# Delta-rule attention before a Fourier-mixing MLP: T V and L U on four array tiles, first blocks from key Gram products, a schedule that counts instruction blocks

## The chip, the cores and the metric

One core of one Trainium2 chip runs the whole program. The metric is device time in microseconds (us). TensorE (PE in the profile; PEld are its weight loads) multiplies, VectorE (DVE), ScalarE (ACT) and GpSimd (POOL) work on elements, and SyncE (SP) issues most DMAs. All data are float32. The profile has two records for each float32 matmul and one for each transpose by TensorE, and each record has a weight load beside it.

## What is computed

```python
# q, k, v: (4, 8, 768, 48); beta: (4, 8, 768); k_n = k / (norm(k) + 1e-6)
for t in range(768):                        # a state of 48 x 48 for each of 4 x 8 heads
    y[:, :, t] = q_t @ state
    state += beta_t * outer(k_n_t, v_t - k_n_t @ state)
x = y, the heads side by side               # (4, 768, 384)
u = x + real(fft(fft(x, axis=1), axis=2))
un = (u - mean(u)) / sqrt(var(u) + 1e-6)    # over the 384
out = u + relu(un @ w_ch1) @ w_ch2          # 384 -> 1536 -> 384
```

## The kernel before

**Units.** The recurrence is done in chunks of 64 tokens. A unit is 128 tokens (two chunks, c = 0 and 1, on partitions 0 to 63 and 64 to 127) of all 8 heads of one batch; 6 units make a batch and 24 the program. A head is h = 2j + s: j counts pairs, and s = 0 (even) or 1 (odd) tells on which half of the partitions the head lies once keys and queries are transposed. Units come in rounds: units 0 to 3, units 4 and 5 (these two rounds are the early ones, batch 0), and then four at a time.

**One unit.** `turn` (line 490) transposes keys and queries with eight 64x64 transposes each. `gram` (line 528) forms K K^T and K Q^T in chunks; the masked K Q^T is L. A triangular inverse T of the key products (with beta and the norms) is formed by row elimination on DVE over 32x32 blocks (`invert`, line 784) for a round at once, and `blocks` (line 814) joins the 32-blocks to 64. For the early rounds the elimination is over 16x16 blocks (`invert16`, line 704), and `join` (line 749) makes 32-blocks of them by matmuls. Their diagonal blocks come from `diag` (line 508), 32x32 products of the transposed keys, which DVE transposes straight out of PSUM in `begin16` (line 636). `ahead` (line 868) makes W^T = K^T T (the copy of `wt`) and U = T V (the copy of `u`). `step` (line 898), for each chunk, subtracts W S from U (DVE, line 922) and adds K^T U to the state S (DVE, line 943): this is the serial chain of a batch, 12 chunk steps long. `outputs` (line 949) sums Q S and L U in PSUM and moves it to `x` (two ACT copies, two DVE adds of line 996).

**Array tiles.** A matmul with 64 rows and 64 columns uses a quarter of the array: rows of half c or s, columns of the PSUM half that it writes. W^T, `gram` and the Q S part of `outputs` use all four quarters in turn. T V and L U use two: chunk c is read on half c and written on half c.

**After attention.** When a batch's last unit is out, `mixing` runs on it: `folds` (DVE), `seq` (matmuls with `tab`), `feat` (matmuls with `ft`, the mean and the variance), `normed` (transposes of `un`), and `mlp`, three groups of 256 tokens with 12 PE operations each of some 2.6 us (line 1172). Batch 0 has no earlier MLP beside its attention; batches 1 to 3 have that of the batch before. The float64 weights come as pairs of 32-bit words and are turned into float32 by ACT, DVE and POOL (`weights`, line 1222), through staging places in `xs[1]` and `R1`.

**Who sets the order.** `Plan` (line 40) collects all operations with a duration, their data dependencies, and a due time. `schedule` plays them through on a model of the engines (four PSUM slots, the DMA rate, the gated TensorE clock) and emits each engine's instructions in the order of that play; on the chip each engine works its list off in order. Between 35 and 123 us of the planned time, when recent TensorE columns are below `TARGET` per us, it lets only big matmuls in, or puts fillers into the list (`idle`, line 1437: a 128x128 by 128x256 matmul whose result nobody reads).

```python
LIM = {"attn": 3, "mix": 2, "mlp": 2}       # PSUM slots a class may hold, of four
t[a, 0, D * h:D * h + D]  <-  z.TT[a, h, :], z.V[a, h, :]     # T V: a = half c
t[a, c, D * h:D * h + D]  <-  z.LT[a, h, :], z.U[a, h, :]     # L U, added to Q S
```

Of the kernel before, what the change touches and what calls it, by code (L numbers as in the profile page):

```python
# [24 lines left out]
class Op:  # L25
    __slots__ = ("i", "engs", "fn", "deps", "succ", "pr", "mode", "banks", "new", "lat",
                 "ndep", "ready", "start", "end", "eng", "due", "kb", "col")


SHARE = 0.6  # L30
# [3 lines left out]
TARGET, SPANW = 350.0, 2.6  # L34


class Plan:
# [10 lines left out]
    def op(self, engs, fn, rd=(), wr=(), pr=0.0, mode=None, new=None, use=(), lat=0.0,  # L48
           due=1e9, kb=0, col=0):
# [4 lines left out]
        o.due, o.kb, o.col = due, kb, col  # L54
# [27 lines left out]
    def speed(self, now):  # L82
# [5 lines left out]
        return 2.0 if self.cold and CLOCK else 1.0  # L88

# [18 lines left out]
    def schedule(self, pick, limits, switch, idle=None, span=(0.0, 0.0)):  # L108
# [24 lines left out]
        self.win, self.sum, self.cold, self.past, self.hist = 0.0, 0.0, True, [], []  # L133
        done, n, now = 0, len(ops), 0.0
        order = []
        while done < n:
            progressed = False
            for e in self.ENG:
# [4 lines left out]
                if e == "PE":  # L143
# [4 lines left out]
                    low = span[0] <= now < span[1] and self.light(now)  # L148
                    if low:
                        cand = [o for o in cand if o.col > 1000]  # L150
# [6 lines left out]
                    if low and best is None and fr and idle:  # L157
                        best = Op()
                        best.i, best.fn, best.mode, best.deps = -1, idle(fr[0]), "128", set()
                        best.pr, best.lat, best.due, best.kb, best.col = 0.0, 0.0, 0.0, 0, 256  # L160
                        best.engs, best.new, best.banks, best.succ = {"PE": 0.22}, None, [], []
                        slots[fr[0]] = now + 0.3
                elif cand:
# [6 lines left out]
                    if best and LOOK and e in ("DVE", "ACT"):  # L170

                        x = now + best.engs[e] - HOLD
                        if any(now < o.ready[e] < x and o.pr < best.pr - LOOK for o in avail[e]
                               if e in o.engs and o is not best):
                            best = None
# [15 lines left out]
                if o.kb:  # L191
# [4 lines left out]
                    o.lat = landed[-1] - o.end  # L196
                free[e] = o.end
# [38 lines left out]
def _consts(S, DM):  # L236
# [10 lines left out]
    lo = (p % 32) >= 16  # L247
    pack = np.concatenate([ident, su, mk.reshape(128, 64), m01, lo[:, None]], axis=1)
# [32 lines left out]
def kernel(  # L281
# [41 lines left out]
    pack = sb("pack", 128 + 64 + 64 + 3)  # L323
# [39 lines left out]
    m16 = pack[:, 258:259]  # L363
    PK = A(pack, 0, 259)
# [6 lines left out]
    def I(x):  # L371
        kp(x)
# [64 lines left out]
    def unit(u):  # L437
# [25 lines left out]
        if u < GS + 2:  # L463
            g, go = w1, 3072 + 256 * u
            z.GF = g[:, go:go + 256].rearrange("p (h t) -> p h t", h=H)
            z.aGF = A(g, go, go + 256)
# [24 lines left out]
    def turn(z, pr, what=(1, 0), after=()):  # L491
# [3 lines left out]
        def fn(e):  # L495
            t = psum(b)
            for i, a in enumerate(what):
                w = (z.Q, z.K)[a].rearrange("p (j s) t -> p j (s t)", s=2)
                for j in range(NJ):
                    for c in range(2):  # L500
                        tr(t[:, c, 256 * a + 64 * j:256 * a + 64 * j + 64],
                           w[64 * c:64 * c + 64, j, :], 64 * c, 64, i == 0 and j == 0)
        rd = [PK] + [(A(z.q, 0, 512), z.aK())[a] for a in what] + list(after)
        P.op({"PE": 0.35 * len(what)}, fn, rd, [(z.aQT, z.aTT)[a]() for a in what], pr, "T",
             new=b, lat=LE, col=500)
        for a in what:
            def ev(e, a=a):
                copy(e, z.QK[:, a].rearrange("p e j t -> p e (j t)"),
                     psum(b)[:, :, 256 * a:256 * a + 256])
            P.op(either(512), ev, [], [(z.aQT, z.aTT)[a]()], pr - EV, use=[b], lat=LA)  # L510

    def diag(z, b, ul, pr):
# [961 lines left out]
```

## Time and profile before

| | us |
|---|---|
| median of 3 runs | 744.56 (744.11 to 747.56) |
| the profiled execution | 751.2 |
| its span in the trace | 749.1 |
| TensorE busy, share of the span | 695.9, 93% |
| VectorE busy | 404.6, 54% |
| ScalarE busy | 243.9, 33% |
| mean granted TensorE clock | 0.969 |
| fillers: records, busy | 102, 34.2 |
| first `join` matmul | 36.7 |
| first state step (`step`) | 63.3 |
| first matmul of batch 0's `seq` | 126.4 |
| first MLP matmul | 152.1 |

The profiled execution is one execution; its span lies inside its time. The profile shows the program by engine, by stretches of time, by the chain of work that ended last, and by groups of instructions under the line that issued them. Most matmuls are issued by the helper at line 375, transposes at 378 and copies at 384, so groups are told apart by the tiles that they read and write: `pp<-u,us` is U as moving operand (K^T U and L U), `pp<-st,us` is Q S, `pp<-us 64*64 64x48` is T V, `pp<-us 64*64 64x64` is W^T. "issue" is time in which an engine waited for nothing that the profile shows. A matmul's record has the time from its start to its modelled end, some 0.2 us, and the next record starts long before that end: the pace is read from how many start in a stretch.

### The profile page before, as it was taken

Reading aid. Unit: us, or ns where it says so; the run is one execution under the profiler, and the core shown is the slowest. Engines: PE = TensorE matmul, PEld = TensorE weight load, DVE = VectorE, ACT = ScalarE, POOL = GpSimd, SP = SyncE. Lnnn points to the kernel's source line nnn. Section 1 sums busy time; section 2 is a strip of 40 time slices with the busy share of each in tenths; the row PEclk is TensorE's granted clock in tenths of the full one; section 3 lists DMA queues with packets and bytes.
Section 4 is the critical chain, followed back from the end, with each engine's and each line's share of the span. In section 5 each row is a group of like instructions: output and inputs, shape, how many; then the busy total and the mean of one; then the engine's idle time right before and its main releaser. Section 6 shows DMA issues by size and latency. Waiting matters only on the chain.

```text
span 749.1 us, 22953 instructions
## 1 busy us (share of the span) xinstructions
PE 695.9 (93%) x10332; PEld 551.2 (74%) x10332; DVE 404.6 (54%) x1074; ACT 243.9 (33%) x546; POOL 28.5 (4%) x31
## 2 busy tenths in 40 slices
PE   4397999989899999898999999999999999999997
PEld 4276888877688676887778767778777677777774
DVE  1984559899533794469943589327992400600000
ACT  3163465633534113354144321255213110421110
POOL 2011211011100000000000000000000000000000
PEclk9998889999899999898999999999999999999999
DMA  9515242210222001320013200010000000000000
GB/s 197 171 27 144 50 111 40 69 57 28 80 67 55 11 21 37 64 55 1 0 25 77 45 11 22 11 46 14 2 1 24 1 22 0 22 1 1 21 22 21
DMA packets 82563, 31.34 MB, mean 42 GB/s; under 512 B 75553, under 2 KB 79618, under 8 KB 82338
## 3 DMA queue, kind: packets, MB, share of 16 engines
q1 hardware_dynamic: 82274, 29.65, 16.2%
q8 instruction: 81, 1.33, 0.8%
q10 hardware_dynamic: 192, 0.23, 0.1%
q14 instruction: 16, 0.13, 0.1%
HBM read 25.16 MB, written 4.72 MB: 40 GB/s over the span
## 4 chain that ended last, share of the span: by engine, by line
PE 68%; DVE 25%; issue 4%; ACT 2%; DMA 1%; SPq 0%; ACTq 0%; DVEq 0%
PE pp L375 62%; DVE rr L800 5%; DVE tmp L795 5%; PE pp L1437 4%; PE pp L378 2%; DVE rr L809 1%; DVE gd L812 1%; DVE pm L1017 1%; DVE un L1136 1%; DVE eo L1017 1%; DVE x L996 1%; ACT x L384 1%; DVE us L822 1%; DMA us<-in_k_dram 1%; DVE rr L610 1%
## 5 line engine op out<-in xcount | busy, mean ns | idle before, releaser
L375 PE MATMUL pp<-w,R 128*128 128x384 f32 x576 | 202.6, 498 | 0.0
L375 PE MATMUL pp<-R,w 128*128 128x256 f32 x864 | 200.6, 386 | 0.8 <-ACT R L384 0.8
L375 PEld LDWEIGHTS pp<-R,w 128*128 128x128 f32 x864 | 164.4, 193 | 30.1 <-ACT R L384 1.0
L375 PEld LDWEIGHTS pp<-w,R 128*128 128x128 f32 x576 | 108.3, 192 | 64.3 <-issue 3.6
L1186 ACT ACTIVATE R<-pp 128x512 f32<-128x512 f32 x72 | 43.0, 597 | 209.8 <-PE pp L375 204.7
L375 PE MATMUL pp<-us 64*64 64x48 f32 (+3 forms) x2368 | 73.2, 250 | 5.5 <-ACT us L384 3.5
L375 PEld LDWEIGHTS pp<-us 64*64 64x64 f32 (+2 forms) x2368 | 63.7, 142 | 13.6 <-issue 8.3
L1214 DVE TENSOR_TENSOR x<-x,pp 128x768 f32<-128x768 f32 x12 | 11.4, 951 | 108.6 <-PE pp L375 108.6
L384 ACT ACTIVATE us<-pp 128x512 f32<-128x512 f32 (+2 forms) x110 | 48.6, 463 | 49.3 <-PE pp L375 32.7
L375 PE MATMUL pp<-u,us 64*64 64x48 f32 x1360 | 57.1, 228 | 2.9 <-issue 2.5
L375 PEld LDWEIGHTS pp<-u,us 64*64 64x64 f32 x1360 | 50.6, 142 | 9.6 <-issue 8.0
L800 DVE TENSOR_TENSOR rr<-rr,tmp 128x30 f32<-128x30 f32 (+9 forms) x150 | 50.6, 337 | 4.4
L795 DVE TENSOR_TENSOR tmp<-rr 128x30 f32<-128x30 f32 (+9 forms) x150 | 50.4, 336 | 4.5
L922 DVE TENSOR_TENSOR u<-u,pp 64x384 f32<-64x384 f32 (+1 forms) x55 | 25.2, 471 | 50.5 <-PE pp L375 40.6
L943 DVE TENSOR_TENSOR st<-st,pp 128x192 f32<-128x192 f32 (+1 forms) x50 | 15.2, 312 | 52.3 <-PE pp L375 45.1
L384 ACT ACTIVATE x<-pp 64x384 f32<-64x384 f32 x48 | 23.3, 485 | 44.0 <-PE pp L375 43.7
L375 PE MATMUL pp<-tab,R 128*96 128x193 f32 (+2 forms) x192 | 35.8, 330 | 0.2 <-DVE x L996 0.2
L384 ACT ACTIVATE R<-pp 128x384 f32<-128x384 f32 (+7 forms) x66 | 23.7, 414 | 32.5 <-PE pp L375 19.7
L1437 PE MATMUL pp<-pack 128*128 128x256 f32 x102 | 34.2, 464 | 0.0
L375 PE MATMUL pp<-st,wt 48*64 48x48 f32 x704 | 32.5, 226 | 1.5 <-DVE st L943 0.7
L375 PEld LDWEIGHTS pp<-tab,R 128*96 128x96 f32 (+2 forms) x192 | 30.2, 163 | 3.6 <-issue 1.7
L375 PEld LDWEIGHTS pp<-st,wt 48*64 48x64 f32 x704 | 27.8, 139 | 6.3 <-issue 5.1
(124 smaller groups left out, 690.0 us busy)
## 6 DMA issues: line engine op xcount, KB each, us to landing
qt<-in_q_dram SPq DMA_DIRECT2D x24, 192.0 KB, 2.9
x<-in_moe_w_ch_dram SPq DMA_DIRECT2D x9, 512.0 KB, 4.4
out_dram<-x SPq DMA_DIRECT2D x12, 384.0 KB, 2.5
us<-in_v_dram SPq DMA_DIRECT2D x22, 192.0 KB, 3.0
us<-in_k_dram SPq DMA_DIRECT2D x22, 192.0 KB, 3.3
tab<-k_tab SPq DMA_DIRECT2D x1, 1155.0 KB, 8.0
R<-in_moe_w_ch_dram SPq DMA_DIRECT2D x3, 384.0 KB, 4.8
x<-in_moe_w_ch_dram SPq DMA_DIRECT2D x3, 384.0 KB, 3.2
```

Of the source, the lines that this page charges most:

```text
L375: I(nc.tensor.matmul(o, lhsT=lhsT, rhs=rhs, start=start, stop=stop, skip_group_check=True))
L378: I(nc.tensor.matmul(o, lhsT=src, rhs=ident[p0:p0 + n, p0:p0 + n], is_transpose=True, start=start, stop=True, skip_group_check=True))
L384: I(nc.scalar.activation(o, i, ACT.Copy, **({} if scale is None else {"scale": scale})))
L610: vec(1400, lambda e: I(nc.vector.transpose(R, ro.gd(0, 4).rearrange("p (n c) -> p c n", c=32))), [ro.agd(0, 4)], [aR], pr)
L795: I(eng(e).tensor_tensor(T_, R[:, :, j + 1:32, j:j + 1].broadcast_to([128, ns, n, j]), R[:, :, j:j + 1, 0:j].broadcast_to([128, ns, n, j]) ...
L800: I(eng(e).tensor_tensor(R[:, :, j + 1:32, 0:j], R[:, :, j + 1:32, 0:j], T_, op=ALU.add))
L922: I(nc.vector.tensor_tensor(U, U, psum(b1)[a, :, s0:s1].rearrange("p s (j d) -> p s j d", d=D), op=ALU.subtract))
L943: I(nc.vector.tensor_tensor(sn[:, s0:s1], so[:, s0:s1], psum(b2)[:, 0, s0:s1], op=ALU.add))
L1017: I(eng(e).tensor_tensor(o, i0, i1, op=op))
L1186: I(nc.scalar.activation(o, psum(bk)[:, :, 0:256], ACT.Relu))
L1214: I(nc.vector.tensor_tensor(w, w, psum(bk)[:, :, 0:DM], op=ALU.add))
L1437: I(nc.tensor.matmul(pst[slot][:, 0, 0:256], lhsT=pack[:, 0:128], rhs=pack[:, 0:256], start=True, stop=True, skip_group_check=True))
```

## The change

- **T V on four quarters.** An odd head's product is written to the other half of the partitions and to a second PSUM bank. U is then moved by three copies (even heads of both halves; the odd heads of each half back to their own half) where one did it before.
- **L U on four quarters.** In the same manner; the odd heads' sums lie apart from Q S, and `outputs` has two copies and three adds in place of two and two.
- **First blocks.** `diag` goes. `keys` makes the whole 64x64 key products of two units in 32 matmuls on four quarters, copies move the diagonal 32-blocks to `gd` (four copies of 32 partitions for two units), and `begin16` transposes from there. The off-diagonal part is kept, so the early rounds' `gram` makes K Q^T alone.
- **`join`** uses 64-row operands with zeros in place of 32-row ones: 16 matmuls where it had 32, and two more masked ACT copies for each of the six units.
- **`turn`** makes four 128x128 transposes where it had eight 64x64, into one bank for each of K and Q.
- **Schedule.** Each PE operation is given its number of instructions `ni`; the model charges 3.4 us for each block of 256 and lets a block be asked for 128 instructions ahead. `TARGET` goes from 350 to 450, and when columns are low anywhere, and not in that window alone, a big matmul is taken first if there is one. `SHARE` (how long ACT must be busy before DVE takes a copy that either may do) goes from 0.6 to 0.3. Two evictions in `feat` get a lower priority. Weights go through other staging places.

```diff
+BLOCK, AHEAD, FETCH = 256, 128, 3.4
-TARGET, SPANW = 350.0, 2.6
+TARGET, SPANW = 450.0, 2.6
+    def fetch(self, o):
+        n0, n1 = self.count, self.count + o.ni
+        for k in range((n0 - AHEAD) // BLOCK + 1, (n1 - AHEAD) // BLOCK + 1):
+            t = o.start + (o.end - o.start) * (k * BLOCK + AHEAD - n0) / o.ni
+            self.come.append(max(t, self.come[-1]) + FETCH)
+        for k in range(n0 // BLOCK + 1, n1 // BLOCK + 1):
+            if k < len(self.come):
+                o.end = max(o.end, self.come[k] + (o.end - o.start) * (n1 - k * BLOCK) / o.ni)
+        self.count = n1
...
-                    low = span[0] <= now < span[1] and self.light(now)
-                    if low:
-                        cand = [o for o in cand if o.col > 1000]
+                    low = self.light(now)
+                    big = [o for o in cand if o.col > 1000] if low else []
+                    low = low and span[0] <= now < span[1]
+                    if low or big:
+                        cand = big
...
     def turn(z, pr, what=(1, 0), after=()):
-                    for c in range(2):
-                        tr(t[:, c, 256 * a + 64 * j:256 * a + 64 * j + 64],
-                           w[64 * c:64 * c + 64, j, :], 64 * c, 64, i == 0 and j == 0)
+                    tr(t[:, i, 128 * j:128 * j + 128], w[:, j, :], 0, 128, j == 0)
...
+    def keys(zs, ro, ul, pr):
+                for j in range(NJ):
+                    for s, c in ((0, 0), (1, 1), (0, 1), (1, 0)):
+                        w = z.QK[64 * s:64 * s + D, 1, c, j, :]
+                        mm(t[64 * c:64 * c + 64, s, i, j, :], w, w, i == 0 and j == 0)
...
     def ahead(z, pr):
-            for h in range(H):
-                for c in range(2):
-                    a = slice(64 * c, 64 * c + 64)
-                    mm(t[a, 0, D * h:D * h + D], z.TT[a, h, :], z.V[a, h, :], h == 0)
+            for j in range(NJ):
+                for s, c in ((0, 0), (1, 1), (1, 0), (0, 1)):
+                    a, x = slice(64 * c, 64 * c + 64), 64 * (c ^ s)
+                    mm(t[x:x + 64, s, D * j:D * j + D], z.TT[a, 2 * j + s, :], z.V[a, 2 * j + s, :],
+                       j == 0)
...
-        P.op(either(DM), lambda e: copy(e, z.ut, psum(b2)[:, 0, 0:DM]), [], [A(z.ut, 0, DM)],
-             pr - EV, use=[b2], lat=LA)
+        def g2(e):
+            copy(e, us[:, 0], psum(b2)[:, 0, 0:W].rearrange("p (j d) -> p j d", d=D))
+        P.op(either(W), g2, [], [A(z.ut, 0, DM)], pr - EV, use=[b2], lat=LA)
+        for c in range(2):
+            def g3(e, c=c):
+                a, x = slice(64 * c, 64 * c + 64), slice(64 - 64 * c, 128 - 64 * c)
+                copy(e, us[a, 1], psum(b2)[x, 1, 0:W].rearrange("p (j d) -> p j d", d=D))
+            P.op(either(W), g3, [], [A(z.ut, 0, DM, 64 * c, 64 * c + 64)], pr - EV, use=[b2],
+                 lat=LA)
...
     def outputs(z, pr):
-            for h in range(H):
-                for c in range(2):
-                    a = slice(64 * c, 64 * c + 64)
-                    go(t[a, c, D * h:D * h + D], c, c, z.LT[a, h, :], z.U[a, h, :])
+            for j in range(NJ):
+                for s, c in ((0, 0), (1, 1), (1, 0), (0, 1)):
+                    h = 2 * j + s
+                    a, y = slice(64 * c, 64 * c + 64), 64 * (c ^ s)
+                    o = D * (h - s * c)
+                    go(t[y:y + 64, c, o:o + D], c, c ^ s, z.LT[a, h, :], z.U[a, h, :])
...
+        for r, s, p, bank, ps in ((hi, 0, hi, 0, 0), (hi, 1, lo, 1, 0), (lo, 1, hi, 0, 1)):
+                I(nc.vector.tensor_tensor(xv(r, s), xv(r, s), pv(p, bank, ps), op=ALU.add))
...
-    weights(moe_w_ch1, w1, KD, DFF, xw, 0)
-    weights(moe_w_ch2, w2, KF, DM, rw + rw + xw + xw + xw[0:1], 0)
+    weights(moe_w_ch1, w1, KD, DFF, [rw[0], xw[0], rw[1], xw[1]], 0)
+    weights(moe_w_ch2, w2, KF, DM, [xw[1], xw[0]], 0)
```

Counted in the two programs' lists of PE instructions (four for a float32 matmul, two for a transpose):

| stretch of the PE list | instructions before, after | fillers before, after |
|---|---|---|
| up to the first `join` | 1036, 608 | 0, 5 |
| first `join` to first state step | 1516, 888 | 19, 12 |
| first state step to first `seq` | 3664, 3548 | 20, 29 |
| first `seq` to first MLP matmul | 456, 380 | 12, 21 |
| from there to the end | 13992, 13768 | 0, 0 |

## The prediction, made before the changed kernel ran

> **What bounds the kernel now.** I read the page's first parts, then the busy time by stretches cut at the marks of the table above, then TensorE's waits, then single stretches of the timeline.
>
> ```profile
> PE 695.9 (93%) x10332; PEld 551.2 (74%) x10332; DVE 404.6 (54%) x1074; ACT 243.9 (33%) x546; POOL 28.5 (4%) x31
> ...
> PE   4397999989899999898999999999999999999997
> ...
> PEclk9998889999899999898999999999999999999999
> ...
> q8 instruction: 81, 1.33, 0.8%
> ```
>
> TensorE is full from the second sixth to the end; no other engine is near. But full is not quick: the clock dips, 34.2 us of it are fillers, and its instructions come by DMA. 10332 records with 10332 weight loads are 20664 instructions in 81 packets, so 255 in each 16 KB. By stretches (busy us of PE, PEld, DVE, ACT, POOL; clock; DMA):
>
> ```profile
> 0.00:36.70 36.70, 14.49 (x520) 12.61 (x522) 20.79 (x95) 10.20 (x18) 4.14 (x12) 1.00 0.78 188
> 36.70:63.30 26.60, 23.25 (x758) 18.75 (x758) 18.56 (x40) 13.42 (x29) 4.23 (x3) 0.90 0.27 65
> 63.30:126.40 63.10, 59.05 (x1834) 51.17 (x1834) 38.79 (x105) 34.52 (x74) 10.32 (x8) 0.91 0.33 80
> 126.40:152.10 25.70, 23.14 (x229) 20.81 (x227) 21.73 (x57) 14.38 (x39) 0.00 (x0) 1.00 0.22 58
> 152.10:749.10 597.00, 575.96 (x6996) 447.84 (x6996) 304.68 (x779) 171.40 (x387) 9.82 (x8) 0.98 0.11 27
> ```
>
> Two regimes. Up to 152.1 us there is no MLP, and TensorE is busy with batch 0's attention, fillers and half clock. After it, 576 of 597 us are TensorE's: there its work is the time. What stops it in the first regime (TensorE's waits, then its timeline):
>
> ```profile
> PE pp L375 <- issue: 15.0, 14, 2.9
> PE pp L375 <- DVE gd L746: 9.1, 1, 9.1
> ```
> ```profile
> 53.94 0.31 PE L375 MATMUL pp<-us,pb 32*32 32x32 f32 x6
> 55.32 0.53 PE L375 MATMUL pp<-us,pb 32*32 32x32 f32 x21 [1.07 <-issue]
> ...
> 59.05 0.63 PE L375 MATMUL pp<-gd,w 32*32 32x32 f32 x26 [2.21 <-issue]
> 59.61 3.78 PE L1437 MATMUL pp<-pack 128*128 128x256 f32 x8
> ```
>
> An operation of 32 small matmuls is cut in two with nothing to wait for. The records of queue 8 explain it: in dense attention its packets come 3.4 to 4 us apart (299.05, 302.57, 306.33), and each stop ends soon after one (53.05 before 55.32, 56.84 before 59.05). So 256 instructions cost at least some 3.4 us; the 3664 of 63.3 to 126.4 are 14.3 blocks, 49 of its 63 us.
>
> **T V and L U.** The pace, from two timeline answers: T V, then Q S and L U.
>
> ```profile
> 387.23 1.11 PE L375 MATMUL pp<-us 64*64 64x48 f32 x31
> ```
> ```profile
> 406.95 0.56 PE L375 MATMUL pp<-st,us 48*64 48x48 f32 x24
> ...
> 407.41 0.80 PE L375 MATMUL pp<-u,us 64*64 64x48 f32 x21
> ```
>
> Less the last record's 0.22 us: T V starts 31 records in 0.89 us, 30 ns each; L U 21 in 0.58, 29 ns; Q S, of the same size on four quarters, 24 in 0.34, 15 ns. Over the trace, first record to first record of the next operation, the medians are T V 0.88 to 0.93, L U 0.89, Q S 0.47. So each falls by 0.41 us. 18 + 18 of them lie in the full regime: **-14.8**. Bounds: nothing, if they stop for instructions instead, and -16.6 at 0.46. I take the row of Q S. In one stretch the new list has 1712 instructions of attention with no big matmul between (1472 before), where blocks and not quarters would bind: four units' gain, 4 x 0.82, **+3.3** back.
>
> **The other terms of the full regime.** Clock: the trace has eight windows of 3.41 us at half speed after 152 us, worth 8 x 1.7 = 13.7 at most. The new rule takes a big matmul when columns are few, but thinner attention makes more such moments: bounds -10 to +7, I take **-3**. `turn`: a pair of 64x64 transposes takes 0.30/4 = 75 ns; a 128x128 one is bounded by that (-4, half as many instructions) and by twice that (+8, twice the columns a quarter-pair hid); half of a 256-column record (215 ns by the MLP's 2.59/12) is 108 ns, x4 = 0.43 against 0.30, x28: **+3**. Copies: U costs one ACT copy of 490 ns before, then by the nearest rows one of 380 (`us<-pp 128x256`) and two of 333 (`ss<-pp 128x193`), +0.55; outputs one add of 352 ns more, +0.35. Those 18 x 0.90 = 16 us lie on engines with 171 and 305 us of 597 busy, and MLP matmuls run meanwhile; if that cover goes, all 16 count. I take **+1**. Sum of the regime: -10.7.
>
> **Before 152 us.** Up to `join` (36.7): 428 instructions fewer, and the stops of 1.12 and 2.89 us there shrink; one V load instead of two (192 KB, 1.0 us at that stretch's 188 GB/s) stands ahead of the first K on SP's queue; against it 12 copies of some 0.6 us on two engines, and `begin16`'s transpose from SBUF (row of line 610: 1.97) for 1.25 from PSUM. DVE's elimination then ends it as before (the 9.1 us wait). **-1**, bounds -4 to +3. `join` to first step: 888 instructions for 1516. At the old 17.5 ns each 15.6 us instead of 26.6, **-11**. Bounds: 0, if the chain join, copy, elimination of units 4 and 5, T V holds it; -15 at 3.4 us for 256. First step to `seq`: 3548 for 3664 at 17.2 ns, **-2**; nine more fillers of 0.43 to 0.6 against eleven T V and L U of 0.41 less. Bounds -14 (47 us of blocks; the chunk chain needs 12 x 3.6 = 43, a full step being 108.72 to 112.30) to +6. `seq` to MLP: nine more fillers in waits for ACT and DVE, **0**, -2 to +5. The weights on POOL, DVE and ACT end behind the first MLP operations in both lists, and their work is the same.
>
> **Sum.** -10.7 - 1 - 11 - 2 = -24.7. The profiled execution would be 751.2 - 24.7 = 726.5 (span about 724). It stands 6.6 above the median of the runs, so the forecast is 744.56 - 24.7 = **720**, with 708 to 728 as its own range.
>
> **Two rules of the Trainium skill.** "TensorEngine Tiling (Array Packing)", Performance Considerations, PSUM Bottleneck: tiling quickens TensorE and not the evacuation, which may then bind. Here ACT and DVE stand at 33% and 54%; by the rule the 16 us above come in and the sum is -10, 735. "Runtime: NRT & Kernel Launch", Instruction fetch mechanics: blocks of 256 instructions, whose crossing is "mostly hidden". The block size agrees with 255; that it is hidden does not, with 15.0 us of stops. By it the 11 us would not come, and the result were 731.
>
> **Rivals.**
> - *The early stage runs at the block rate* (0.15). For: packets 3.4 us apart, and a schedule that knows them. Against: copies and DVE lie in that chain. -14.8 and -14 in place of -11 and -2: **704**.
> - *Instructions were not what held the early stage* (0.18). For: DVE is busy 18.6 of 26.6 us there and fillers stay in. -11 and -2 go: **733**.
> - *The quarters do not overlap* (0.07), as the odd heads' writes go to other banks and halves. Against: W^T writes in the same pattern in 0.50 us. -14.8 + 3.3 go: **731 to 736**.
> - *Slower: evacuation holds the PSUM slots* (0.10). Attention may hold three slots of four. T V's is held for three copies, the outputs' for five moves. If TensorE stands for them, 24 x 0.55 + 23 x 0.35 = 21 us, and columns get rare enough for one half-clock window in every second of 18 units, 9 x 1.7 = 15. 720 + 36 = **756**. It decides once stops and windows together pass the 24.7 gained. Against: only 21 us of TensorE's 597 are idle now, and stops over 0.25 us behind ACT's copies are 2.4 of them.
>
> **How the numbers follow.** Forecast 0.50. The range leaves out the slower rival and the part of the first below 702: **702 to 741**. About 0.5% can be told from no change, 740.8 to 748.3. Faster 0.88 (forecast, first three rivals but for 0.02 of the second); same 0.04 (that tail and a mild slower case); slower 0.08.
>
> **What would show it.** T V and L U at 15 ns a record, their operations at 0.45 to 0.5; if 30, the third rival. First step near 51 and first MLP matmul near 138; if the first step is past 60, the second rival; if the MLP starts before 128, the first. TensorE's `issue` waits under 15 us. ACT near 265 us busy. Stops of TensorE behind `u` or `x` copies over 10 us, or more than eight half-clock windows after the MLP's start, would speak for the slower one. Wrong in whole if the MLP starts early but attention of batches 1 to 3, tied to DVE's elimination, leaves TensorE idle later.

## The result, and the profile after

The changed kernel takes **750.86 us** (median of 20 executions, 742.38 to 757.6). The kernel before, beside it on the same chip, takes 746.02 (20 executions, 743.58 to 750.35). The ratio is 1.0047, interval 1.0024 to 1.0070: no change, or slightly slower, where 720 us was forecast. In all ratios, executions more than 1.5% above the fastest of their kernel are left out, so a ratio can differ from that of the two medians (most of all in e15 below, where 8 of 12 are).

The profiled execution of the changed kernel is its best, 742.38 us (span 740.6); that of before, 751.2, lies above its median. So the traces differ by -8.5 us where the medians differ by +4.8. A second profile of the same program (e1 below) came out at 755.3. The two have the same instruction lists, and 14.7 us between them is the size of what has to be told apart from the change itself.

The page after, its busy line, TensorE and its clock in 40 slices, and the instruction queue:

```profile
PE 686.2 (93%) x9596; PEld 538.9 (73%) x9596; DVE 437.8 (59%) x1145; ACT 250.8 (34%) x580; POOL 29.7 (4%) x28
...
PE   5479999998999997888999999999999999999997
...
PEclk9589999999999999997999999999999999999999
...
q8 instruction: 75, 1.23, 0.7%
```

TensorE's records fell by 736, its busy time only from 695.9 to 686.2 us. VectorE rose by 33 us; ScalarE, for which 265 was forecast, stands at 250.8, since the lower `SHARE` gave its copies to VectorE (with the old one, in e7 below, the two stand at 416 and 267). The same stretches as before the change (busy us of PE, PEld, DVE, ACT, POOL; clock; DMA), with the marks at the new times:

```profile
0.00:41.03 41.03, 18.14 (x304) 15.28 (x305) 25.12 (x101) 20.00 (x38) 5.53 (x9) 0.77 0.67 167
41.03:60.28 19.25, 19.25 (x445) 16.36 (x446) 11.24 (x30) 10.87 (x26) 1.29 (x1) 0.88 0.06 13
60.28:120.08 59.80, 57.90 (x1783) 49.33 (x1780) 45.44 (x124) 40.10 (x91) 10.66 (x8) 1.00 0.42 103
120.08:147.55 27.47, 25.86 (x192) 23.00 (x190) 22.58 (x62) 11.99 (x33) 1.30 (x1) 1.00 0.16 47
147.55:740.60 593.05, 565.00 (x6886) 434.94 (x6884) 333.41 (x831) 167.84 (x394) 10.91 (x9) 0.98 0.11 28
```

The same view of the second profile, from the first `join` on:

```profile
40.56:60.73 20.17, 20.17 (x444) 16.97 (x446) 11.25 (x30) 10.90 (x26) 1.28 (x1) 0.83 0.07 13
60.73:126.50 65.77, 62.39 (x1782) 52.60 (x1779) 45.14 (x124) 40.31 (x91) 10.61 (x8) 0.92 0.38 93
...
153.93:755.30 601.37, 575.53 (x6886) 444.29 (x6884) 333.52 (x831) 168.16 (x394) 10.94 (x9) 0.96 0.11 28
```

Read the clock column. VectorE and ScalarE are busy for the same time, stretch by stretch, to 0.4 us; TensorE's busy time differs by 15.9 us after the first `join`. Time at half clock is 2 x (1 - clock) x length; with the clock's own records in place of its two digits that is 31 us in the first profile (4.8 + 25.8) and 70 us in the second (6.8 + 10.2 + 52.6). The profile with 39 us more at half clock is 15 us longer.

What stops TensorE (its longest waits in the first profile: total, times, longest):

```profile
PE pp L393 <- DVE t L854: 6.9, 6, 2.3
PE pp L393 <- ACT R L402: 6.3, 3, 5.5
PE pp L393 <- ACT us L402: 6.0, 2, 5.5
PE pp L393 <- issue: 5.4, 6, 1.7
```

Waits for instructions fell from 15.0 to 5.4 us, as expected, and all of it ahead of the first MLP matmul: there from 11.1 to 1.5, behind it 3.9 in both. The two waits of 5.5 us lie before the first `join`.

| | forecast, us | first profile | second profile |
|---|---|---|---|
| up to the first `join` | -1 | +4.3 | +3.9 |
| `join` to first state step | -11 | -7.4 | -6.5 |
| first step to `seq` | -2 | -3.3 | +2.7 |
| `seq` to first MLP matmul | 0 | +1.7 | +1.7 |
| from there to the end | -10.7 | -4 | +4.4 |
| sum | -24.7 | -8.5 | +6.2 |

All against the profile of before. T V and L U together did what was forecast: from the first record of each operation to the first of the next, the 18 + 18 of the full regime took 39 us before and 23 and 24 in the two profiles. (In the medians L U came down from 0.96 to 0.47 us, as forecast, and T V from 1.02 to 0.67.) So the question is where some 15 us went in the full regime, and 5 at the start.

### The profile page after: what moved, and what is told of

It reads as the page before. It is cut to its first block, busy times and chain, and to the rows that moved or that the text cites. A ratio compares the mean times of both kernels' runs of the same rounds, so it can differ in the third digit from the quotient of the medians.

```text
span 740.6 us, 21536 instructions
## 1 busy us (share of the span) xinstructions
PE 686.2 (93%) x9596; PEld 538.9 (73%) x9596; DVE 437.8 (59%) x1145; ACT 250.8 (34%) x580; POOL 29.7 (4%) x28
## 4 chain that ended last, share of the span: by engine, by line
PE 66%; DVE 26%; ACT 4%; issue 3%; DMA 1%; ACTq 0%; DVEq 0%
PE pp L393 58%; DVE tmp L821 5%; DVE rr L826 5%; PE pp L1493 4%; PE pp L396 3%; DVE x L1051 1%; DVE gd L838 1%; ACT R L402 1%; DVE us L586 1%; ACT x L402 1%; DVE us L848 1%; DVE rr L639 1%; DVE rr L835 1%; ACT us L402 1%; DVE pm L1071 1%
## 5 line engine op out<-in xcount | busy, mean ns | idle before, releaser
L393 PE MATMUL pp<-us 64*64 64x64 f32 (+3 forms) x2240 | 57.4, 246 | 8.4 <-ACT us L402 5.5
L393 PEld LDWEIGHTS pp<-us 64*64 64x64 f32 (+1 forms) x2240 | 49.2, 144 | 15.7 <-issue 6.8
L402 ACT ACTIVATE us<-pp 32x256 f32<-32x256 f32 (+2 forms) x101 | 44.4, 452 | 39.8 <-PE pp L396 27.1
L393 PE MATMUL pp<-u,us 64*64 64x48 f32 x1360 | 42.1, 219 | 2.5 <-issue 1.1
L1493 PE MATMUL pp<-pack 128*128 128x256 f32 x134 | 40.6, 428 | 3.1 <-DVE us L586 2.4
L393 PEld LDWEIGHTS pp<-u,us 64*64 64x64 f32 x1360 | 36.3, 134 | 9.7 <-issue 5.8
L402 ACT ACTIVATE pb<-pp 32x256 f32<-32x256 f32 x48 | 18.1, 376 | 45.7 <-PE pp L393 44.7
L1165 DVE TENSOR_TENSOR mx<-pp,ss 128x193 f32<-128x193 f32 x24 | 8.5, 354 | 41.6 <-ACT ss L402 41.6
L393 PEld LDWEIGHTS pp<-st,wt 48*64 48x64 f32 x704 | 26.0, 136 | 8.4 <-issue 6.0
L402 ACT ACTIVATE R<-pp 128x384 f32<-128x384 f32 (+9 forms) x58 | 21.7, 407 | 26.6 <-PE pp L396 13.8
```

What stands on the lines that cost most here:

```text
L393: I(nc.tensor.matmul(o, lhsT=lhsT, rhs=rhs, start=start, stop=stop, skip_group_check=True))
L402: I(nc.scalar.activation(o, i, ACT.Copy, **({} if scale is None else {"scale": scale})))
L1165: I(nc.vector.tensor_tensor(mx[:, 0:hd + 1], psum(bk)[:, 0, 0:hd + 1], ss, op=ALU.add))
L1493: I(nc.tensor.matmul(pst[slot][:, 0, 0:256], lhsT=pack[:, 0:128], rhs=pack[:, 0:256], start=True, stop=True, skip_group_check=True))
```

## Theories

**A**: the clock. The work shrank as forecast, thinner attention makes half-clock stretches, and these give the gain back. **B**: the copies behind T V and L U hold the work. **C**: the other parts (first blocks, turns, planner rules) took the gain. At first I held A, because the two profiles of one program differ by the clock alone.

## Experiments on the parts

Ratios are to the kernel before on the same chip, with intervals; medians in us.

**e1: the changed kernel once more.**

> The changed kernel unaltered, profiled once more and timed beside the kernel before on the same chip. Theory A (TensorE's work did shrink by about 16 us at T V and L U, and typical executions give the gain back as half-clock windows): ratio 1.00 to 1.007, the times spread over 10 us or more, and if this profiled execution is near 750 us its mean granted clock is near 0.95 instead of the 0.966 of the first profile, with the lost time (one minus the clock, times the span) 6 to 12 us larger. Theory B (the copies behind T V and L U hold the work, whatever the clock): a profiled time near 750 with the clock at 0.966 and idle time of TensorE behind the copies of u and x of over 10 us. Theory C (the start and the smaller steps took the gain: first join +4.3 us, turns of q and k +4.6 us): the same milestones as in the first profile within 1 us up to the first MLP matmul.

749.95, ratio 1.0027 (0.9994 to 1.0060). Clock 0.940 in the profile, milestones as above. It agrees with A and with C's start; no stop of 10 us behind copies, so nothing for B.

**e2: T V and L U alone.** Before, with `ahead` and `outputs` of the changed kernel:

```diff
-                    mm(t[a, 0, D * h:D * h + D], z.TT[a, h, :], z.V[a, h, :], h == 0)
+                    mm(t[x:x + 64, s, D * j:D * j + D], z.TT[a, 2 * j + s, :], z.V[a, 2 * j + s, :], j == 0)
...
-                    go(t[a, c, D * h:D * h + D], c, c, z.LT[a, h, :], z.U[a, h, :])
+                    go(t[y:y + 64, c, o:o + D], c, c ^ s, z.LT[a, h, :], z.U[a, h, :])
```

> Only T V and L U on four tiles with their copies, everything else as before, the old schedule rules included. Theory A: T V and L U lose 14 to 17 us in the full regime, and half of it or more comes back as lost clock: ratio 0.985 to 1.0. Theory B: the copies of u and x end TensorE's idle time for over 10 us: ratio 1.0 to 1.02. Theory C (what took the gain is in the other two parts): ratio 0.978 to 0.985, 730 to 735 us.

752.81, ratio 1.0001 (0.9964 to 1.0037), executions from 742 to 762. The full regime's T V and L U fell to 24 us, and the time did not move: A looked confirmed.

**e3: the planner's rules alone.** Before, with `Plan`, `SHARE`, `TARGET`, the two priorities and the weights' places of the changed kernel:

```diff
-SHARE = 0.6
+SHARE = 0.3
-TARGET, SPANW = 350.0, 2.6
+TARGET, SPANW = 450.0, 2.6
+                if e == "PE" and o.ni:
+                    self.fetch(o)
...
-    weights(moe_w_ch1, w1, KD, DFF, xw, 0)
+    weights(moe_w_ch1, w1, KD, DFF, [rw[0], xw[0], rw[1], xw[1]], 0)
```

> Only the new rules of the planner (instruction blocks counted, large matmuls first wherever a window is light, target 450, half the share for due work, the copies of the projections earlier, the weights through four buffers), with the old products. It tells what the schedule part is worth alone. Theory A: neutral in TensorE's work, time 740 to 748 us. Theory C: if the rules move the large matmuls badly, 750 to 765 us. If the rules are what gained in the early stage, first state step earlier than 63 us and the first MLP matmul at 140 to 147 us, total 735 to 742.

764.61, ratio 1.0233 (1.0190 to 1.0275). In it one MLP matmul waits 18.3 us for a VectorE copy (below, e18). Dearer than any theory had it.

**e4: all new products, old rules.**

```diff
-SHARE = 0.3
+SHARE = 0.6
-TARGET, SPANW = 450.0, 2.6
+TARGET, SPANW = 350.0, 2.6
-                    low = self.light(now)
-                    big = [o for o in cand if o.col > 1000] if low else []
-                    low = low and span[0] <= now < span[1]
-                    if low or big:
-                        cand = big
+                    low = span[0] <= now < span[1] and self.light(now)
+                    if low:
+                        cand = [o for o in cand if o.col > 1000]
-                if e == "PE" and o.ni:
+                if False:
-        vec(hd, g1, [A(ss, 0, 1)], [A(mx, 0, hd + 1)], pr - 10, use=[bk])
+        vec(hd, g1, [A(ss, 0, 1)], [A(mx, 0, hd + 1)], pr - EV, use=[bk])
```

> The changed kernel's products with the old planner rules (no counting of instruction blocks, large matmuls first only inside the window where fillers run, target 350, share 0.6, the projections' copies at their old place). Theory A: the clock part stays, 745 to 755 us. If the new rules carried the gain of the early stage, it is slower than the changed kernel by 3 to 8 us; if they cost in the full regime (fewer fillers under target 450 leave more half-clock windows), it is faster by 3 to 8 us, 742 to 747.

**737.45**, ratio 0.9863 (0.9828 to 0.9899): the products are a gain, and the list that the new rules make takes 1.66% of it (12 us; 1.0027 in e1 against 0.9863). The step that A says nothing of is the largest so far. (Two parts of the schedule are not in it. The counting of instruction blocks changes nothing: with the counting taken out of the changed kernel, every engine's list is the same, instruction for instruction. And e4 keeps the weights' new places.)

**e6: the first blocks alone**, with the old T V, L U and rules (e4 with `ahead` and `outputs` of before):

```diff
-                    mm(t[x:x + 64, s, D * j:D * j + D], z.TT[a, 2 * j + s, :], z.V[a, 2 * j + s, :], j == 0)
+                    mm(t[a, 0, D * h:D * h + D], z.TT[a, h, :], z.V[a, h, :], h == 0)
```

> The new first blocks (and their 128 x 128 transposes) with the old T V and L U and the old planner rules. With both products changed and the old rules it is 737.5, with T V and L U alone 748.9 against 748.8 before. If the gain of the pair lies in the first blocks alone: 736 to 740. If the two parts add (each half): 742 to 746 us. If the start and the dearer transposes eat it: 748 to 753.

777.55, ratio 1.0372 (1.0323 to 1.0422), with a stop of 21.8 us of the same kind as in e3, and 83 us of half clock after the first MLP matmul. The parts do not add: alone 1.0001 and 1.0372, together 0.9863.

**e9, e10, e13: two tiles or four, everything else equal.** In the orders of e2, e4 and the changed kernel, the products go back to two tiles, with as many copies and the same lists (each head's product lands on its own half, so the copies no longer cross, and one of the three adds of `outputs` works on the result alone):

```diff
-                    a, x = slice(64 * c, 64 * c + 64), 64 * (c ^ s)
-                    mm(t[x:x + 64, s, D * j:D * j + D], z.TT[a, 2 * j + s, :], z.V[a, 2 * j + s, :],
+                    a = slice(64 * c, 64 * c + 64)
+                    mm(t[a, s, D * j:D * j + D], z.TT[a, 2 * j + s, :], z.V[a, 2 * j + s, :],
...
-                    go(t[y:y + 64, c, o:o + D], c, c ^ s, z.LT[a, h, :], z.U[a, h, :])
+                    go(t[a, c, D * h:D * h + D], c, c, z.LT[a, h, :], z.U[a, h, :])
```

> The kernel that changed only T V and L U, with exactly its order, its copies and its number of instructions, but with the products back on two tiles (each head's product lands on the half it came from; one add per unit works on the result alone). Its four-tile twin took 752.8 us with a lost clock of 34 us in the median. Theory A (the four tiles shorten TensorE's work and the clock takes it back): T V and L U longer by 15 to 19 us in the full regime, lost clock 10 to 18 us smaller, total 750 to 757, within 0.7% of the twin. Theory B (the copies hold the work): the same time as the twin, within 3 us, with the clock unchanged. Theory C (the shorter products count in full and other things took it): 765 to 772.

> The same exchange in the kernel with all new products and the old planner rules (737.45 us): its order and copies, T V and L U back on two tiles. If four tiles are worth in this order what the records say, 750 to 756 us with the lost clock within 3 us; if the clock takes back part, 742 to 748 and a lost clock 8 us smaller; if the copies behind them set the pace, 736 to 740.

> The changed kernel in its very order, T V and L U back on two tiles (same copies; one add per unit works on the result alone). Theory A (the clock takes back what the shorter products give): TensorE's records of both grow by 15 us, the lost clock falls from 36 to 25 us or less, and the time is 750 to 757, within 1% of the changed kernel. If four tiles are worth as much here as with the old rules (10.5 us): 759 to 763, and then the 12 us between the changed kernel and the one with the old rules come from the rules alone.

| order of | two tiles | four tiles | worth |
|---|---|---|---|
| e2 (old first blocks, old rules) | e9: 758.27, 1.0055 (1.0020 to 1.0091) | 752.81, 1.0001 | 0.5%, 4 us (the intervals overlap) |
| e4 (new first blocks, old rules) | e10: 747.91, 0.9957 (0.9928 to 0.9987) | 737.45, 0.9863 | 0.9%, 7 us |
| the changed kernel | e13: 769.15, 1.0278 (1.0239 to 1.0318) | 749.95, 1.0027 | 2.5%, 19 us |

TensorE's timeline of one unit, L U and then W^T and T V, in the changed kernel:

```profile
389.58 0.93 PE L393 MATMUL pp<-u,us 64*64 64x48 f32 x42
...
390.47 1.15 PE L393 MATMUL pp<-us 64*64 64x64 f32 x61
```

and in e13:

```profile
409.37 1.39 PE L393 MATMUL pp<-u,us 64*64 64x48 f32 x45
...
410.77 1.45 PE L393 MATMUL pp<-us 64*64 64x64 f32 x57
```

With the last record's 0.22 us off, L U and the K^T U beside it start a record every 17 ns against 26.

**A does not hold for the changed kernel.** In its own order the four tiles are worth 19 us, about what 2 x 24 operations of 0.41 us make (19.7), and the lost clock of all executions, (1 - clock) x span in the median, is 40 us with two tiles and 36 with four. In the two other orders the gain falls short: 7 us in e4's, with 26.5 us lost against 23.5, and 4 us in e2's, with 34.4 against 22.7. So my reading of e2, that thinner products bring the half clock, fits that order and not the one that was to be explained. B falls too: e9 has as many copies without the shorter products and is 0.55% above before (at most 0.9%), which sets the copies together with e2's change of order at 4 us.

**e11, e14: the old turns**, eight 64x64 transposes, in e4's and in the changed kernel's very order.

```diff
-                    tr(t[:, i, 128 * j:128 * j + 128], w[:, j, :], 0, 128, j == 0)
+                    for c in range(2):
+                        tr(t[:, c, 256 * a + 64 * j:256 * a + 64 * j + 64],
+                           w[64 * c:64 * c + 64, j, :], 64 * c, 64, i == 0 and j == 0)
```

> The kernel with all new products and the old planner rules (737.45 us), in its very order, with the turns of q and k as eight 64 x 64 transposes again. In the full regime the turns took 13 to 14 us in place of 9.3. If that is TensorE time on the path: 731 to 734 us. If the 128 x 128 form only fills time that the work waits anyway: 736 to 739.

> The changed kernel in its very order, with the turns as eight 64 x 64 transposes. With the old rules this gave 5 us (737.45 to 732.38) and a lost clock of 15 in place of 26 us. Expected: 743 to 746 if it carries over, 748 to 752 if the clock or the order hides it.

e11: **732.38**, ratio 0.9768 (0.9734 to 0.9803), 0.96% below e4. e14: 744.67, ratio 0.9926 (0.9890 to 0.9962), 1.0% below the changed kernel. By the ratios the 128x128 turn costs 7 us in either order, by the medians 5. (The lost clock of 26 us in e4 and 15 in e11, which the expectation of e14 sets side by side, cannot be compared: the record of the clock begins at 12.2 us in e4's profile and at 35.0 in e11's; see the last section.) The groups of TensorE's transposes (busy, mean ns), in e4:

```profile
L394 PE MATMUL pp<-pack,qt 128*128 128x128 f32 x96 | 16.8, 310 | 0.0
L394 PE MATMUL pp<-pack,us 128*128 128x128 f32 x88 | 16.1, 318 | 0.0
```

and in e11:

```profile
L394 PE MATMUL pp<-pack,qt 64*128 64x64 f32 x192 | 10.7, 239 | 0.0
L394 PE MATMUL pp<-pack,us 64*128 64x64 f32 x176 | 10.7, 252 | 0.2 <-issue 0.2
```

Half the records, 11.5 us more busy time. These means mix both clocks. Behind the first MLP matmul the median record takes 273 ns in e4 and 222 in e11, and the operations of 0.30 to 0.34 us take 0.49 to 0.53.

**e12: the start.** e11 with the `gd` copies of a pair of units on one engine.

```diff
-            P.op(either(512), g, [], [A(gd0, 1024 * ro.i + 256 * ul, 1024 * ro.i + 256 * ul + 512,
+            e = "ACT" if ul == 0 else "DVE"
+            P.op({e: either(512)[e]}, g, [], [A(gd0, 1024 * ro.i + 256 * ul, 1024 * ro.i + 256 * ul + 512,
```

> The former, and the eight copies of key products into the blocks (gd) put on one engine for each pair of units (ScalarE for the first, VectorE for the second), so that the pairs run beside one another and not in turn. If the serial chain of gd copies is what brought the first join 3 to 4 us later (41.0 against 36.7), it comes at 36 to 38 us and the total is 2 to 4 us below the former: 728 to 732. If the join waits for something else, 39 to 41 us and 731 to 736. The order on TensorE differs from the former after the 18th operation, so a part of any difference may be the order's.

792.12, ratio 1.0477 (1.0429 to 1.0525): another order with the long stop, 26.4 us. The first `join` came at 39.65, not at 36 to 38. The chain of copies is real, as VectorE's timeline in the changed kernel shows,

```profile
13.49 0.68 DVE L404 COPY gd<-pp 32x512 f32<-32x512 f32 x1 [6.82 <-ACT gd L402]
...
16.04 0.69 DVE L404 COPY gd<-pp 32x512 f32<-32x512 f32 x1 [0.52 <-ACT gd L402]
17.38 1.92 DVE L683 STREAM_TRANSPOSE rr<-gd 128x1024 f32<-128x1024 f32 x1 [0.66 <-ACT gd L402]
```

where each copy waits for the other engine's, 4 us in a row. But in e12 the transpose started at 15.94 instead and the elimination's first product at 25.89 (26.55 in the changed kernel, 22.66 before): VectorE is busy for 15 of the 16 us from 23 to 39 in all of them. What is late is VectorE's whole list: the first transpose starts 1 to 3 us later than before (14.94 there), and two transposes take 1.9 us for 1.25 each. The copies that VectorE makes itself are some 1 us of it: in e4 and e11, where ScalarE makes them, VectorE has 22 us of work up to the first `join` in place of 25, and the `join` still comes at 40.14 and 39.26. This is read from the timelines; no run takes the transposes or the copies away.

## Experiments on the rules

One rule undone at a time in the changed kernel:

```diff
# e5: as in e4, large matmuls first only in the fillers' window
# e7
-SHARE = 0.3
+SHARE = 0.6
# e8
-    D0, D1 = 35.0, 123.0
+    D0, D1 = 35.0, 700.0
# e15
-TARGET, SPANW = 450.0, 2.6
+TARGET, SPANW = 350.0, 2.6
# e16
-        vec(hd, g1, [A(ss, 0, 1)], [A(mx, 0, hd + 1)], pr - 10, use=[bk])
+        vec(hd, g1, [A(ss, 0, 1)], [A(mx, 0, hd + 1)], pr - EV, use=[bk])
```

(e8 undoes none, it allows fillers everywhere; e16 changes the sister line as well.)

> The changed kernel, with large matmuls preferred only inside the stretch where fillers run (the old rule). The order on TensorE differs only after the first MLP matmul. If this rule cost the 12 us between the changed kernel and the one with all old rules: 738 to 742 us, clock 0.96 to 0.97. If it had no part in it: 748 to 752, clock 0.94 to 0.966 as for the changed kernel.

> The changed kernel with the old threshold at which VectorE takes a copy that ScalarE could do (ScalarE busy for 0.6 us more, not 0.3). VectorE's busy time should fall from 438 to about 418 us and ScalarE's rise from 251 to about 267. If VectorE's extra copies hold up the early stage: 738 to 743 us. If they do not matter: 748 to 752.

> The changed kernel with fillers allowed in the whole run and not only up to 123 us of the planner's time: 140 fillers instead of 67. Theory A (thin stretches at half clock eat what T V and L U gave): the clock rises to 0.975 or more, the spread of the times falls to a few us, and the time is 738 to 745 us. Theory B or C (copies, start, smaller steps): the fillers only cost, some 10 us, 755 to 762 us.

> The changed kernel with the old threshold for a light stretch (350 in place of 450 columns a us): 47 fillers in place of 67, and large matmuls are preferred less often. If the higher threshold costs by spending large matmuls and 20 fillers early: 738 to 745. If it protects the clock: 752 to 758 with a lost clock above 40 us.

> The changed kernel with the two VectorE copies of each projection at their old, more urgent place in the planner. If their later place delayed the projections and let the clock fall behind them: 740 to 746. If it has no part: 748 to 753.

| | median | ratio |
|---|---|---|
| e5: old rule for large matmuls | 761.33 | 1.0155 (1.0100 to 1.0211) |
| e7: share 0.6 | 751.37 | 0.9964 (0.9919 to 1.0008) |
| e8: fillers everywhere | 755.87 | 1.0059 (1.0021 to 1.0096) |
| e15: target 350 | 762.53 | 1.0022 (0.9976 to 1.0068) |
| e16: projections' copies | 753.12 | 1.0048 (1.0009 to 1.0088) |

None gives the 12 us back. The rule for large matmuls is worth 1.1 to 1.3% as it stands (its expectation had it as a cost), the share costs 0.6 to 0.8% (5 to 6 us; the interval touches e1's and is clear of the first measurement's), and the others cannot be told from nothing. The share is also seen at the start. From the first `join` to the first state step, e7 has as many TensorE records as the changed kernel's first profile (445), a full clock, and 2 us less:

```profile
39.82:57.04 17.22, 17.22 (x445) 14.35 (x445) 12.03 (x32) 11.61 (x28) 1.30 (x1) 1.00 0.20 53
```

The first state step comes at 56.0 to 57.7 us in the profiles with the new first blocks and a share of 0.6 (e4, e6, e7, e10, e11, e17; only e12, with its `gd` copies tied to engines, has 60.0), and at 59.6 or later in all with 0.3.

e8 does not decide on A. Its profile has 3.4 us of half clock after the first MLP matmul, where the changed kernel's two have 26 and 53, and the kernel is no faster, as 33 us of TensorE's time there go to fillers. But 33 us more work made it only 1 to 2 us slower by the ratios and 5 by the medians, so the clock that it won back, or idle time that the fillers stood in, must have been worth most of them.

Then one new rule at a time on top of e11:

```diff
# e17
-                    low = span[0] <= now < span[1] and self.light(now)
-                    if low:
-                        cand = [o for o in cand if o.col > 1000]
+                    low = self.light(now)
+                    big = [o for o in cand if o.col > 1000] if low else []
+                    low = low and span[0] <= now < span[1]
+                    if low or big:
+                        cand = big
# e18
-SHARE = 0.6
+SHARE = 0.3
```

> The kernel with all new products, the old turns and the old rules (732.4 us), with one new rule added: large matmuls first in every light stretch of the run. In the changed kernel this rule was worth 11 us (761 without it). If that carries over: 722 to 729 us with a lost clock of 15 us or less. If the rule only mends what the other new rules do: 730 to 735. If it is one of the rules that cost: 738 or more.

> The same base (732.4 us) with the share at 0.3: VectorE takes a copy as soon as ScalarE is busy for 0.3 us more. VectorE's busy time should rise by some 15 to 20 us. If the share is the costly rule: 738 to 746 us, with the first state step 2 to 3 us later than 57.6. If not: 730 to 735. If the new order puts a VectorE copy that frees an MLP matmul's bank behind the second elimination: 750 or more, with one stop of 15 us or more near 175 us.

e17 (large matmuls first everywhere): 732.54, ratio 0.9834 (0.9780 to 0.9889), the same median as e11 and a ratio 0.7% higher, with overlapping intervals: no gain. e18 (share 0.3): **800.95**, ratio 1.0717 (1.0648 to 1.0787). One threshold, from 0.6 to 0.3 us, costs 69 us, by the long stop that the last case of its expectation named and by much half clock. The stretches of e18 from the first `join`:

```profile
40.63:64.91 24.28, 24.28 (x376) 19.93 (x378) 13.72 (x31) 10.13 (x24) 1.33 (x1) 0.50 0.11 21
64.91:138.15 73.24, 69.86 (x1824) 60.01 (x1823) 44.95 (x120) 39.31 (x90) 10.55 (x8) 0.71 0.33 81
...
166.62:804.30 637.68, 585.70 (x6990) 458.87 (x6990) 332.89 (x830) 164.77 (x389) 11.45 (x9) 0.91 0.10 26
```

and of e11:

```profile
39.26:57.63 18.37, 18.36 (x478) 15.60 (x480) 12.01 (x32) 11.50 (x28) 1.28 (x1) 0.91 0.17 43
57.63:115.34 57.71, 54.47 (x1736) 46.01 (x1733) 41.94 (x112) 37.57 (x87) 7.82 (x6) 0.94 0.35 79
...
144.33:731.40 587.07, 558.98 (x6996) 429.88 (x6996) 317.94 (x799) 181.54 (x430) 12.22 (x10) 0.98 0.12 29
```

In e18 TensorE runs at half clock through all of the first of these stretches (0.50) and most of the second (0.71), and the last stretch is 51 us longer. The last stretch has one long stop; TensorE's timeline and VectorE's, around 196 us of e18:

```profile
175.13 0.40 PE L394 MATMUL pp<-pack,un 64*128 64x64 f32 x6 [0.69 <-ACT R L1240]
196.36 1.22 PE L391 MATMUL pp<-R,w 128*128 128x256 f32 x2 [20.82 <-DVE us L586]
```
```profile
194.25 0.19 DVE L826 TENSOR_TENSOR rr<-rr,tmp 128x30 f32<-128x30 f32 x1
194.48 1.22 DVE L835 TENSOR_TENSOR rr<-rr,gb 128x1024 f32<-128x1024 f32 x1
195.62 0.68 DVE L586 TENSOR_TENSOR us<-pp,pack 128x512 f32<-128x512 f32 x1
```

The MLP matmul needs the PSUM slot of a `gram`, and the masking of that `gram` (L586) stands in VectorE's list behind the whole elimination of a round. The same stop is in e3 (18.3 us), e6 (21.8) and e12 (26.4), behind the same masking, and in none of the others. In three of these four (e6, e12, e18), 83 to 124 us after the first MLP matmul are at half clock; in e3, 46.

## Why the prediction was wrong

- **T V and L U (-14.8, +3.3 back, copies +1).** The mechanism held, and in the changed kernel the size too: 15 to 16 us in the records, 19 in the time (e13). In e4's and e2's orders the same edit is worth 7 and 4 us. The Trainium skill, "TensorEngine Tiling (Array Packing)", Performance Considerations, PSUM Bottleneck, warns that the evacuation may bind when tiles are packed; here it does not: by e9 the copies and the order that came with them are 4 us, and in the changed kernel's first profile TensorE waits 0.6 us in all behind the moves of `u` and `x`.
- **Turns (+3).** They cost 7 us (e11, e14). The bounds, -4 to +8, held it. 0.43 us was taken for the operation; it takes 0.49 to 0.53, and the early 20 of them count too, which the sum left out.
- **Up to the first `join` (-1).** +4 (+3.4 in e4). Twelve copies were named and priced as hidden; the stretch is VectorE's, which the prediction saw (the 9.1 us wait for L746) and did not follow: the dearer transposes, 2 x 0.7 us, and the copies that they wait for are on the path.
- **`join` to first step (-11).** -7.4 and -6.5. TensorE never stands in this stretch (busy 19.25 us of 19.25, 20.17 of 20.17), so on the chip its list and its clock set the length. 4.8 and 6.8 us are at half speed, and 7.6 us of the first profile's go to the 12 fillers, which the planner put where its model had nothing to run (12.7 us and 19 before). Where the clock is full throughout (e4, e7, e10) the stretch takes 16.9 to 17.2 us, 9.4 to 9.8 less than before. The 17.5 ns for an instruction were not far off: e7's 17.2 us are 19 ns. The first step so came at 60.2 and 60.7, just past the 60 that were to speak for the second rival (instructions did not hold the early stage). That rival is not right for it: the waits for instructions went, and with them most of the gain came; the late `join` and the half clock moved the step. "Runtime: NRT & Kernel Launch" of the Trainium skill, Instruction fetch mechanics, holds block crossings to be mostly hidden; the waits of 15.0 us that became 5.4 with 75 packets for 81 say that in the stretches of small matmuls here they were not.
- **The failing step: the planner's rules.** They entered the sum as "clock, -3", with bounds of -10 to +7 and one rule of five in mind. `SHARE` was not priced at all, and nothing was allowed for the order. The list that they make costs 12 us (e4), outside those bounds. With this +12 in place of -3, the turns at 7 in place of 3, and the start and the stretch from `join` to step as they are in e4 (+3.4 in place of -1, -9.8 in place of -11), the sum reads -24.7 + 15 + 4 + 4.4 + 1.2 = -0.1, with +2 to +3.5 measured by the ratios. That the terms meet so well is partly luck: the early turns count in the turns' 7 and in the start, and e9, e10 and e13 give 4, 7 and 19 us for one and the same edit.
- **The slower rival** had the right second half (half-clock stretches) for a wrong cause (copies holding PSUM slots). Its marks, stops behind `u` or `x` copies over 10 us or more than eight half-clock windows, were partly met: no such stops, but 26 and 53 us (8 and 15 windows) at half clock after the MLP's start in the two profiles, against 29 before.

What stays open: by which path the new list costs 12 us, and whether the rules as such cost it or this one order. Smaller changes moved the time by more through the order: eight copies tied to engines by 7% (e12 against e11), one threshold by 9.7% (e18). Of the rules the share is the only one that costs in both tests: 0.6 to 0.8% in the changed kernel, about half of the 12 us, and the 9.7% on e11. That the new target and the rule for large matmuls hide the rest of its cost in the changed kernel is a guess; for it speaks that with target 350 (e15) 31 us from the first `join` to `seq` are at half clock, against 5 and 17. No pair of rules was tried. For the clock as the path speaks that the median lost clock of all executions is 26.5 us in e4 and 36 in the changed kernel, with records that begin within 3 us of each other. At 0.7 to 0.8 us of time for each us of lost clock, as the changed kernel's own executions have it, that is 7 to 8 of the 12 us; this is an estimate from one line through scattered times, and what lowered the clock is not shown.

The best order found is e11 (732.38) or e17 (732.54), some 2% below the kernel before: the new products and first blocks, the old turns, the old share.

## What to carry to other kernels

When an edit passes through a planner or any list scheduler, price the list and not the edit: keep one build with the new work in the old order and one with the old work in the new order, since here the two parts had opposite signs and hid one another. A gain that "vanished into the clock" in one order was whole in another, so one order is not enough to blame the clock. Before a short stretch is put down to a chain, look whether the engine idles in it at all: from `join` to the first step it did not: fillers and half clock were a good part of it. And on in-order engines look for the copy that frees a bank behind a long chain: one such place stopped TensorE for 18 to 26 us in four orders.

## What the hardware showed

- **Half clock can last while TensorE is busy.** In e2, TensorE is at half clock from 507 to 528 us, after attention in which it was busy for 8.5 of 10 us, and stays there while it is busy all the time (three stretches in a row):

```profile
495.00:505.00 10.00, 8.54 (x363) 7.46 (x362) 3.59 (x6) 7.11 (x18) 0.00 (x0) 1.00 0.24 63
505.00:512.00 7.00, 6.71 (x136) 6.27 (x135) 3.77 (x10) 2.65 (x7) 0.00 (x0) 0.66 0.16 33
512.00:519.00 7.00, 7.00 (x93) 6.45 (x94) 4.15 (x13) 2.97 (x8) 0.00 (x0) 0.50 0.00 0
```

  In the second profile of the changed kernel a dip at 290 us lasts 27 us; in the first, at the same place of the list, 3.4. Executions of this one program spread by 15 us, and among the executions of a kernel the time moves by 0.4 to 1.1 us for each us of lost clock.
- **The record of the clock begins late** (at 40.8 us in before, 11.7 after), and the time ahead of it counts as full speed. It was not: the transposes of queries in the kernel before take 311 ns at 19 us, where its row has the clock at 1.00, and 222 later (min/median/max):

```profile
L378 PE MATMUL pp<-pack,qt x16: 311/311/366, 19.3 to 20.1; 64*128 64x64 f32 x16
L378 PE MATMUL pp<-pack,qt x112: 222/222/223, 223.1 to 511.6; 64*128 64x64 f32 x112
```

  So the mean clocks of kernels that begin differently (0.969 before, 0.966 after) are not comparable, nor is the first row of the stretches.
- **A copy of 32 partitions costs what one of 128 does**: 0.59 us on ScalarE for 32x512, 0.60 for 128x512 (the changed kernel, 12 to 13 us). Four quarter copies are four copies.
- **VectorE's 128x1024 transpose** takes 1.92 us from SBUF (the changed kernel, L683) and 1.25 from PSUM (before, L660).
